# The first expert's list taken from its counts again, and two digits of the second search ahead of the expert matmuls

## The chip, the cores and the metric

The kernel runs on one core of a Trainium2 chip. The metric is the device time of one execution in microseconds (us): the median of three runs. The engines are TensorE (PE in the profile, PEld for its weight loads), VectorE (DVE), ScalarE (ACT), GpSimd (POOL), and SyncE (SP), which issues DMAs here.

## The reference, cut to what matters

Two blocks, one behind the other. The first is a linear recurrence over 768 steps for 4 batches and 8 heads of 48 elements. Its output, 3072 tokens of 384 elements, goes to a layer of eight experts, in which every expert takes exactly 384 tokens. The tokens are given out greedily: all 3072 x 8 scores are sorted, and each token goes to its best expert that still has a place.

```python
def _moe_ref(x, w_gate, w1, w2):
    N, D = x.shape                      # 3072, 384
    E = w_gate.shape[1]                 # 8
    cap = N // E                        # 384
    logits = x @ w_gate
    order = np.argsort(-logits.flatten())
    assigned = -np.ones(N, dtype=np.int64)
    counts = np.zeros(E, dtype=np.int64)
    for idx in order:
        tok, e = (int(idx) // E, int(idx) % E)
        if assigned[tok] >= 0 or counts[e] >= cap:
            continue
        assigned[tok] = e
        counts[e] += 1
        ...
    for e in range(E):
        mask = assigned == e
        h = np.maximum(x[mask] @ w1[e], 0.0)
        out[mask] = h @ w2[e]
```

## The kernel before: the parts concerned

The attention block runs in steps, with the routing's constants made beside it in small pieces. Then the kernel fills one expert in each round. A round searches for the level of the score at which the first expert is full, in five digits of four bits, from the highest to the lowest; gives that expert its tokens; makes a list of them; gathers their rows; and queues that expert's matmuls. The expert matmuls of the list before are taken from the queue `pe_work` in small portions, between the search's own small matmuls, so that TensorE isn't idle while VectorE works. In the first round there is nothing queued, and idle matmuls (`idle_turns`) stand in the gaps.

A digit is counted in one of two ways. `digit_alone` needs 24 small matmuls (4 in the first round's first digit) and few operations of VectorE. `digit_beside` needs 3 matmuls and one more, and more operations of VectorE, and takes expert matmuls from the queue in two portions, `slots`.

```python
def digit_alone(above, parts, choice, unit, counted=None, turns=(0, 0), scored=None):
    some(pe_work, turns[0])
    r = bank("cnt", "r")
    ...                                            # the counts: 24 matmuls
    fills = rt([E], "fills", BF16)
    tt(fills[0:NTH, :], r[0:NTH, 0:E], ..., ALU.is_ge)
    filled = rt([1], "filled", BF16)
    reduce(filled[0:NTH, :], fills[0:NTH, :], ALU.max)
    if turns[1]:
        some(pe_work, turns[1])
        idle_turns(2, bank("nothing", "O"))
    digit = r[:, 128:129]
    nc.tensor.matmul(out=digit, lhsT=unit[0:NTH, :], rhs=filled[0:NTH, :], start=True, stop=True)
    if scored:
        scores, n = scored
        nc.tensor.matmul(out=scores[:, 0:E], lhsT=weights[n][:], rhs=fills[0:NTH, :],
                         start=(n == 0), stop=(n == len(weights) - 1), skip_group_check=True)
    return digit, ALU.add

def digit_beside(above, choice, size, slots):
    some(pe_work, slots[0])
    ...                                            # cnt: 3 matmuls
    some(dve_work, 1)
    ...                                            # own, part, parts
    some(pe_work, slots[1])
    ...                                            # cnt: 1 matmul; fillsb, filledb, sized and digit
```

After the search the expert's tokens are marked. The first round does it in its own way, the others with `assign`:

```python
def assign(choice, over, pick, slots):
    over, level = over
    stt(sure[:], col(over[:], E), level, choice[:], ALU.is_ge, ALU.mult)
    reduce(count[:], by_e(sure), ALU.add)
    some(pe_work, slots[0])
    r = bank("sums", "r")
    nc.tensor.matmul(out=r[:, 0:E], lhsT=ones[:], rhs=count[:], start=True, stop=True)
    some(pe_work, slots[1])
    take(over[:], pick, level)                     # new, taken
    tt(places[:], places[:], r[:, 0:E], ALU.subtract)

def assign_first(choice, over, pick, scores):
    over, level = over
    reduce(top[:], scores[:, 0:E], ALU.max)
    stt(named[:], scores[:, 0:E], top[:], first[:], ALU.is_equal, ALU.mult)
    reduce(m[:], named[:], ALU.max)
    stt(taken[:], over[:], level, pick[:], ALU.is_ge, ALU.mult)
    def marked():
        stt(sure[:], col(over[:], E), level, choice[:], ALU.is_ge, ALU.mult)
    def counted():
        ...                                        # count, its matmul (sums), places
    return m, marked, counted
```

The list: `members` names the expert that is full (m) and its tokens, `place` numbers them, `index` computes the number e, on which the load of the weights depends, `lines` and `in_line` sort the tokens into lines, and `tokens` ends in three gathers by GpSimd. The first list's rows (xe) are transposed by TensorE into xeT; those of the later lists by DMA, between copies of GpSimd.

```python
def members():
    ...
    named = m
    if named is None:
        stt(score[:], places[:], 0.5, left[:], ALU.is_lt, ALU.mult)
        reduce(named[:], score[:], ALU.max)
    ts(member[:], taken[:], named[:], ALU.is_equal)

for rnd in range(E - 1):
    slots, more = pace.get(rnd, (4, 2)), 3 if rnd > 1 else -2 if rnd and not exact else 0   # pace: rounds 1, 2: (3, 2)
    ...
    scores = bank("scores", "H") if rnd == 0 else None
    over = search(choice, over, digits, slots, more, counted, ((1, 1),) if rnd == 1 else (), scores)
    if rnd or exact:
        (assign_exact if exact else assign)(choice, over, pick, (3, 3))
        *pieces, used = expert_list(rnd == 0)
    else:
        m, marked, after = assign_first(choice, over, pick, scores)
        *pieces, tokens, used = expert_list(True, m=m)
        pieces += [marked, tokens, after]
    dve_work.extend(pieces)
    while dve_work:
        some(dve_work, 1)
        if rnd: some(pe_work, 1)
        elif dve_work: idle_turns(1, bank("nothing", "O"))
    close()                                        # full, penalty
    if rnd == 0:
        idle_turns(13, bank("nothing", "O"))
        dve_work.append(lambda: also(bank("hits", "r")))   # the range check, taken up in the next search
```

Of the kernel before, what the change touches and what calls it, by code (L numbers as in the profile page):

```python
# [11 lines left out]
FP32 = mybir.dt.float32  # L12
FP32R = mybir.dt.float32r
BF16 = mybir.dt.bfloat16
# [13 lines left out]
def kernel(  # L28
# [32 lines left out]
    nc = tc.nc  # L61
# [520 lines left out]
    taken = rt([NT], "taken", FP32, 1)  # L582

    lowest = rt([E], "lowest", FP32, 1)
    lowlogit, digits, weights = const([128, 1], FP32, "lowlogit"), [], []

    def bounds(c1):

# [36 lines left out]
        def table(shift):  # L625
            steps = const([128, NTH], FP32, f"steps_{shift}")
            ts(steps[:], count[:, 0:NTH], step[:], ALU.mult, float(1 << shift), ALU.mult)
            unit = const([128, 128], BF16, f"unit_{shift}")

            ts(unit[:], ones[:], step[:], ALU.mult, float(1 << shift) * (-1 if shift else 1),  # L630
               ALU.mult)
            digits.append((steps, unit, steps[:, 0:1]))
            weight = const([NTH, 128], BF16, f"weight_{shift}")
            nc.vector.memset(weight[:], float(1 << shift))
            weights.append(weight)

        def negated():
            ts(pair[:, 1:2], pair[:, 1:2], -1.0, ALU.mult)
# [81 lines left out]
    def assign_and_run(begun=None, also=None, again=None, exact=None):  # L720
# [57 lines left out]
            else:  # L778
                stt(above[:, c0:c1], over, digit, steps, op, ALU.is_ge)

        def digit_alone(above, parts, choice, unit, counted=None, turns=(0, 0), scored=None):

            some(pe_work, turns[0])
            r = bank("cnt", "r")
            cols = [c for c in range(NT) if not counted or c % NCH == NCH - 1]
            for c in cols:
                if c % 8 == 0 and not counted:
                    parts(c, c + 8)
                nc.tensor.matmul(out=r[0:NTH, 0:E], lhsT=above[:, c, :], rhs=choice[:, c, :],
                                 start=(c == cols[0]), stop=(c == cols[-1]))  # L790
# [52 lines left out]
        def search(choice, over, digits, slots, first=0, counted=None, alone=(), scores=None):  # L843


            def less(over, digit, op):
# [7 lines left out]
            for n, (steps, unit, size) in enumerate(digits):  # L854
                above = counted[0] if counted else rt([NT, NTH], "above", BF16)
                parts = partial(reached, above, over, digit, op, steps)
                if slots and n >= len(alone):
                    parts(0, NT)
                    new = less(over, digit, op)
                    digit, op = digit_beside(above, choice, size, (slots[0] + first, slots[1]))  # L860
                    over = new
                else:
                    new, op_new = digit_alone(above, parts, choice, unit, counted,
                                              *(alone[n:n + 1] or ((0, 0),)),
                                              scored=(scores, n) if scores is not None else None)
                    over = less(over, digit, op)
                    digit, op = new, op_new
                if n >= len(alone):
                    first = 0
                counted = None  # L870
            return less(over, digit, op) if exact else (over, digit)

        def assign(choice, over, pick, slots):
# [10 lines left out]
            some(pe_work, slots[1])  # L884
            take(over[:], pick, level)
            tt(places[:], places[:], r[:, 0:E], ALU.subtract)

        def assign_first(choice, over, pick, scores):

            over, level = over  # L890
            top, named, m = rt([1], "top_"), rt([E], "named"), rt([1], "m")
            reduce(top[:], scores[:, 0:E], ALU.max)
            stt(named[:], scores[:, 0:E], top[:], first[:], ALU.is_equal, ALU.mult)
            reduce(m[:], named[:], ALU.max)
            stt(taken[:], over[:], level, pick[:], ALU.is_ge, ALU.mult)
            sure = rt([NT, E], "sure", BF16)

            def marked():
                stt(sure[:], col(over[:], E), level, choice[:], ALU.is_ge, ALU.mult)

            def counted():
                count = rt([E], "count", BF16)
                with nc.allow_low_precision("counts of at most 24"):
                    reduce(count[:], by_e(sure), ALU.add)
                r = bank("sums", "r")
                nc.tensor.matmul(out=r[:, 0:E], lhsT=ones[:], rhs=count[:], start=True, stop=True)
                tt(places[:], places[:], r[:, 0:E], ALU.subtract)

            return m, marked, counted

        def assign_exact(choice, over, pick, slots):
            def take_all(mask):
# [39 lines left out]

            stt(wanted[:], full[:], 2.0 * N, places[:], ALU.mult, ALU.add)

        def expert_list(alone=False, last=False, m=None):

            L = {"place": next(turns), "last": last}

# [6 lines left out]
            def members():  # L965
                if alone:

                    L["xe"] = [rows() for _ in range(TE)]
                    for xe in L["xe"]:
                        nc.gpsimd.memset(xe[0:1, 0:1], 0.0)  # L970
                named = m
                if named is None:
                    score, named = rt([E], "score"), rt([1], "m")
                    stt(score[:], places[:], 0.5, left[:], ALU.is_lt, ALU.mult)
                    reduce(named[:], score[:], ALU.max)
                member = rt([NT], "member")
                ts(member[:], taken[:], named[:], ALU.is_equal)
                L.update(member=member, m=named)

            def place():  # L980
                incl = rt([NT], "mincl", BF16)
# [189 lines left out]
        with tc.manual_schedule(engines=engines):  # L1171
# [3 lines left out]

            pace, settle = {0: None, 1: (3, 2), 2: (3, 2)}, []
            for rnd in range(E - 1):
                slots, more = pace.get(rnd, (4, 2)), 3 if rnd > 1 else -2 if rnd and not exact else 0
                if exact:
                    best, pick, masked = picks()  # L1180
                    choice = choices_exact(pick, masked)
# [11 lines left out]
                else:  # L1193
# [234 lines left out]
```

## Time and profile before

| what | value |
|---|---|
| median of 3 runs | 449.82 us (449.33 to 450.61) |
| span in the profile | 448.2 us |
| mean granted TensorE clock | 0.979 |
| TensorE busy | 426.6 us, 95% |
| VectorE busy | 274.0 us, 61% |
| DMA | 63.25 MB, mean 141 GB/s |

The page divides the span into 40 slices of 11.2 us. A digit is the busy share of a slice in tenths; PEclk is the granted TensorE clock in the same way.

```profile
PE   8999999999999678998999999999999999999994
DVE  6789977778987677766666567567567562000000
PEclk9999999999999859999999999999999999999999
```

Thirteen slices are the attention. In the next two or three, where the first list is searched and made, TensorE has little to do and its clock falls; the rest is the experts' matmuls with the later searches among them. The largest groups of instructions are the two kinds of expert matmuls (L1141 and L1153), 264 us together.

### The profile page before, as it was taken

The numbers are of one execution on the slowest core, as the hardware profiler recorded it, in microseconds if no ns is written. First come the engines' busy times: TensorE is split into PE (matmuls) and PEld (weight loads), VectorE is DVE, ScalarE is ACT, GpSimd is POOL, SyncE is SP. The second block draws the span as 40 slices with busy tenths as digits, with TensorE's granted clock in tenths as the row PEclk, the third lists the DMA queues.
The fourth block names the chain that finished last, engine by engine and source line by source line (L and its number), as shares of the span: only waits on it lengthen the run. The fifth ranks groups of instructions, "written<-read, shape, count | busy, mean of one in ns | idle before, by whom it ended". The sixth has DMA issues, their size and how long they took to land. (4 is left out here: it accounts for less than half of the span.)

```text
span 448.2 us, 11779 instructions
## 1 busy us (share of the span) xinstructions
PE 426.6 (95%) x4806; PEld 287.2 (64%) x4806; DVE 274.0 (61%) x887; ACT 129.3 (29%) x302; POOL 174.9 (39%) x231
## 2 busy tenths in 40 slices
PE   8999999999999678998999999999999999999994
PEld 5788988898888535554565565565565565555552
DVE  6789977778987677766666567567567562000000
ACT  4666665666552101200210210210210211211210
POOL 2566555565551021036146037037037037531001
PEclk9999999999999859999999999999999999999999
DMA  9999998999811136084194093093093096820001
GB/s 158 180 165 191 195 189 181 207 196 199 182 38 39 37 114 221 1 303 99 38 333 72 35 335 86 20 332 78 31 333 88 19 332 169 293 56 35 0 20 39
DMA packets 135200, 63.25 MB, mean 141 GB/s; under 512 B 118464, under 2 KB 129760, under 8 KB 135136
## 3 DMA queue, kind: packets, MB, share of 16 engines
q1 hardware_dynamic: 132016, 52.91, 47.6%
q0 software_dynamic: 3072, 9.44, 5.8%
q8 instruction: 40, 0.66, 0.6%
q14 instruction: 24, 0.20, 0.1%
q10 hardware_dynamic: 48, 0.05, 0.1%
HBM read 48.77 MB, written 9.49 MB: 130 GB/s over the span
## 5 line engine op out<-in xcount | busy, mean ns | idle before, releaser
L1141 PE MATMUL H<-xeT,w 128*128 128x384 f32 x384 | 131.9, 495 | 1.6 <-POOL xeT L1110 1.5
L1141 PEld LDWEIGHTS H<-xeT,w 128*128 128x128 f32 x384 | 69.3, 190 | 45.9 <-issue 5.4
L1153 PE MATMUL O<-w,hT 128*128 128x384 f32 x192 | 66.5, 492 | 0.0
L1153 PE MATMUL last_O<-w,hT 128*128 128x384 f32 x192 | 66.1, 491 | 0.0
L1145 ACT ACTIVATE hT<-H 128x384 f32<-128x384 f32 x64 | 31.4, 491 | 104.2 <-PE H L1141 102.8
L1153 PEld LDWEIGHTS last_O<-w,hT 128*128 128x128 f32 x192 | 35.4, 190 | 22.6 <-issue 0.9
L1153 PEld LDWEIGHTS O<-w,hT 128*128 128x128 f32 x192 | 35.1, 190 | 22.9 <-issue 2.0
L327 DVE COPY_PREDICATED am<-mask,A 128x512 f32<-128x512 int32 x48 | 32.2, 724 | 17.5 <-PE A L322 17.5
L193 POOL TENSOR_TENSOR low<-g,upper 128x384 fp32r<-128x384 f32 x22 | 22.3, 1013 | 43.4 <-DVE upper L191 40.2
L1030 POOL TENSOR_TENSOR block<-past 128x72 f32<-128x72 f32 x8 | 2.5, 306 | 88.3 <-DVE at L570 77.5
L1072 POOL DMA_INDIRECT xe<-xd,token x21 | 21.4, 1020 | 26.1 <-DVE full L567 15.8
L337 PE MATMUL Y<-v,am 128*64 128x48 f32 x768 | 27.8, 223 | 1.2 <-DVE am L327 1.1
L1158 POOL DMA_INDIRECT out_dram<-o,token x21 | 21.8, 1037 | 16.9 <-ACT o L1157 12.8
L1110 POOL COPY xeT<-cols 128x768 uint16<-128x768 uint16 x21 | 22.2, 1066 | 14.0 <-DMA cols<-parts 13.9
L337 PEld LDWEIGHTS Y<-v,am 128*64 128x64 f32 x768 | 24.8, 138 | 2.3 <-DVE am L327 1.9
L246 POOL TENSOR_TENSOR kg<-k,ek 128x384 f32<-128x384 f32 x23 | 23.1, 1004 | 7.2 <-ACT ek L224 5.4
L322 PE MATMUL A<-qT,kT 48*64 48x128 f32 x768 | 25.7, 272 | 0.0
L1100 POOL COPY parts<-xe 128x768 uint16<-128x768 uint16 x21 | 17.4, 855 | 17.0 <-DMA xe<-xd,token 14.4
L1157 ACT COPY o<-O 128x384 f32<-128x384 f32 x12 | 5.7, 479 | 61.1 <-PE O L1153 45.5
L223 ACT ACTIVATE eq<-dl 128x384 f32<-128x384 f32 x24 | 12.5, 523 | 31.7 <-DVE dl L221 31.7
L1157 ACT COPY o<-last_O 128x384 f32<-128x384 f32 x11 | 5.3, 479 | 55.3 <-PE last_O L1153 35.5
L322 PEld LDWEIGHTS A<-qT,kT 48*64 48x64 f32 x768 | 20.9, 133 | 0.4 <-issue 0.3
(238 smaller groups left out, 683.3 us busy)
## 6 DMA issues: line engine op xcount, KB each, us to landing
w<-in_moe_w_dram SPq DMA_DIRECT2D x16, 1536.0 KB, 7.0
f<-in_f_logit_dram SPq DMA_DIRECT2D x24, 192.0 KB, 4.0
q<-in_q_dram SPq DMA_DIRECT2D x24, 192.0 KB, 4.6
k<-in_k_dram SPq DMA_DIRECT2D x24, 192.0 KB, 4.7
v<-in_v_dram SPq DMA_DIRECT2D x24, 192.0 KB, 4.7
xd<-x SPq DMA_DIRECT2D x24, 192.0 KB, 3.8
xe<-xd,token POOLq DMA_INDIRECT x21, 4.9
cols<-parts SPq DMA_TRANSPOSE x21, 2.8
```

What stands on the lines that cost most here:

```text
L193: nc.gpsimd.tensor_tensor(out=low[:], in0=g[:, :, 0:DH], in1=upper[:].bitcast(FP32), op=ALU.subtract)
L246: engine.tensor_tensor(out=G["kg"][:, :, 0:DH], in0=G["k"][:], in1=G["ek"][:], op=ALU.mult)
L322: nc.tensor.matmul(out=A[par][HC * j:HC * j + HC, 128 * hp:128 * hp + 128], lhsT=G["kT"][rows, hp, HC * j:HC * j + HC], rhs=G["qT"][rows, ...
L327: nc.vector.copy_predicated(am[:, par], mask[:].unsqueeze(1).to_broadcast((128, HP, 128)), A[par][:].rearrange("s (a t) -> s a t", t=128))
L337: nc.tensor.matmul(out=Y[par][HC * j:HC * j + HC, DH * hp:DH * hp + DH], lhsT=G["am"][:, par, hp, HC * j:HC * j + HC], rhs=G["v"][:, 2 * h ...
L1072: nc.gpsimd.indirect_dma_start(out=xe[:], out_offset=None, in_=xd[:, :], in_offset=bass.IndirectOffsetOnAxis(ap=token[:, i:i + 1], axis=0))
L1100: nc.gpsimd.tensor_copy(out=rows[-1][:], in_=xe[:].bitcast(U16).rearrange("t (d h) -> t h d", h=2))
L1110: nc.gpsimd.tensor_copy(out=halves[:, :, :, 128 * i:128 * i + 128], in_=t[:].rearrange("p (h c) t -> p h c t", h=2))
L1141: nc.tensor.matmul(out=L["H"][:, 0:CAP], lhsT=L["w1"][:, d, 128 * ft:128 * ft + 128], rhs=xT[:, d, :], start=(d == 0), stop=(d == DC - 1))
L1145: nc.scalar.activation(out=hT[:, ft, :], in_=L["H"][:, 0:CAP], func=AF.Relu)
L1153: nc.tensor.matmul(out=L["O"][:, 0:D], lhsT=hT[:, ft, 128 * i:128 * i + 128], rhs=L["w2"][:, ft, :], start=(ft == 0), stop=(ft == FC - 1))
L1158: nc.gpsimd.indirect_dma_start(out=outs[next(tiles)][:, :], out_offset=bass.IndirectOffsetOnAxis(ap=L["token"][:, i:i + 1], axis=0), in_=o ...
```

## The change

The change takes the first list's special way out. The first round's expert is no longer named from sums of the digits' comparisons (`scores`, with the five constants `weight`), but as in the later rounds from the places that are left, which `assign` counts ahead of the list; so the counting stands ahead of the list again and not behind it. In the second round two digits of the search are counted with `digit_alone`, with the portions (0, 1) and (1, 1) of the queue, where before it was one with (1, 1); and the third digit takes 3 + 2 from the queue, where before the second took 3 - 2 = 1 and then 2. What it is for: fewer parts and one way for all rounds, and one digit less among the expert matmuls.

```diff
-    lowlogit, digits, weights = const([128, 1], FP32, "lowlogit"), [], []
+    lowlogit, digits = const([128, 1], FP32, "lowlogit"), []
...
-            weight = const([NTH, 128], BF16, f"weight_{shift}")
-            nc.vector.memset(weight[:], float(1 << shift))
-            weights.append(weight)
...
-        def digit_alone(above, parts, choice, unit, counted=None, turns=(0, 0), scored=None):
+        def digit_alone(above, parts, choice, unit, counted=None, turns=(0, 0)):
...
-            fills = rt([E], "fills", BF16)
+            fills = rt([E], "fills")
...
-            if scored:
-
-                scores, n = scored
-                nc.tensor.matmul(out=scores[:, 0:E], lhsT=weights[n][:], rhs=fills[0:NTH, :],
-                                 start=(n == 0), stop=(n == len(weights) - 1),
-                                 skip_group_check=True)
...
                     new, op_new = digit_alone(above, parts, choice, unit, counted,
-                                              *(alone[n:n + 1] or ((0, 0),)),
-                                              scored=(scores, n) if scores is not None else None)
+                                              *alone[n:n + 1])
...
-                if n >= len(alone):
-                    first = 0
-                counted = None
+                first, counted = 0, None
...
-        def assign_first(choice, over, pick, scores):
-            ...                                                   (the whole function)
...
-                named = m
-                if named is None:
-                    score, named = rt([E], "score"), rt([1], "m")
-                    stt(score[:], places[:], 0.5, left[:], ALU.is_lt, ALU.mult)
-                    reduce(named[:], score[:], ALU.max)
+                score, m = rt([E], "score"), rt([1], "m")
+                stt(score[:], places[:], 0.5, left[:], ALU.is_lt, ALU.mult)
+                reduce(m[:], score[:], ALU.max)
...
-                slots, more = pace.get(rnd, (4, 2)), 3 if rnd > 1 else -2 if rnd and not exact else 0
+                slots, more = pace.get(rnd, (4, 2)), 3 if rnd > 1 else 0
...
-                    scores = bank("scores", "H") if rnd == 0 else None
                     over = search(choice, over, digits, slots, more, counted,
-                                  ((1, 1),) if rnd == 1 else (), scores)
-                if rnd or exact:
-                    (assign_exact if exact else assign)(choice, over, pick, (3, 3))
-                    *pieces, used = expert_list(rnd == 0)
-                else:
-                    m, marked, after = assign_first(choice, over, pick, scores)
-                    *pieces, tokens, used = expert_list(True, m=m)
-                    pieces += [marked, tokens, after]
+                                  ((0, 1), (1, 1)) if rnd == 1 else ())
+                (assign_exact if exact else assign)(choice, over, pick, (3, 3))
+                *pieces, used = expert_list(rnd == 0)
```

In the order of TensorE's instructions the change moves these: the five matmuls for `scores` go; the matmul for `sums` moves from behind the tokens to ahead of the list; 24 small count matmuls, two idle matmuls and one digit's matmul come in among the three transposes of the first list's rows; and the range check's matmul (`hits`) stands behind three expert matmuls instead of ahead of all.

More of the change, by code (lines that the diff above doesn't have):

```diff
@@ L841, in digit_beside, with search @@
             return digit[:], ALU.subtract
-        def search(choice, over, digits, slots, first=0, counted=None, alone=(), scores=None):
+        def search(choice, over, digits, slots, first=0, counted=None, alone=()):
             def less(over, digit, op):
@@ L886, in assign @@
             tt(places[:], places[:], r[:, 0:E], ALU.subtract)
-        def assign_first(choice, over, pick, scores):
[L890 to L909, printed above, removed]
         def assign_exact(choice, over, pick, slots):
@@ L953, in closed, with expert_list @@
             stt(wanted[:], full[:], 2.0 * N, places[:], ALU.mult, ALU.add)
-        def expert_list(alone=False, last=False, m=None):
+        def expert_list(alone=False, last=False):
             L = {"place": next(turns), "last": last}
@@ L970, in members @@
                         nc.gpsimd.memset(xe[0:1, 0:1], 0.0)
-                named = m
-                if named is None:
-                    score, named = rt([E], "score"), rt([1], "m")
-                    stt(score[:], places[:], 0.5, left[:], ALU.is_lt, ALU.mult)
-                    reduce(named[:], score[:], ALU.max)
+                score, m = rt([E], "score"), rt([1], "m")
+                stt(score[:], places[:], 0.5, left[:], ALU.is_lt, ALU.mult)
+                reduce(m[:], score[:], ALU.max)
                 member = rt([NT], "member")
-                ts(member[:], taken[:], named[:], ALU.is_equal)
-                L.update(member=member, m=named)
+                ts(member[:], taken[:], m[:], ALU.is_equal)
+                L.update(member=member, m=m)
             def place():
```

## The prediction

> **What bounds the kernel now.** The page's busy table comes first: TensorE is busy for 95% of the span, VectorE for 61%. The chain that ended last says nothing here (it covers only the last queue's closing steps), so the stages have to be cut by hand from the slices and then measured with the table of windows. Its columns are span, busy time and count of PE, PEld, DVE, ACT and POOL, then granted clock, DMA share and GB/s.
>
> ```profile
> PE 426.6 (95%) x4806; PEld 287.2 (64%) x4806; DVE 274.0 (61%) x887; ACT 129.3 (29%) x302; POOL 174.9 (39%) x231
> ...
> 160.40:166.20 5.80, 4.04 (x33) 1.45 (x34) 5.32 (x20) 0.00 (x0) 1.29 (x2) 0.50 0.30 82
> 166.20:175.00 8.80, 7.13 (x58) 3.95 (x56) 6.41 (x29) 1.44 (x3) 3.32 (x4) 0.81 0.91 321
> 175.00:209.30 34.30, 34.02 (x147) 19.31 (x146) 23.87 (x90) 4.96 (x11) 8.42 (x10) 1.00 0.45 140
> 209.30:210.90 1.60, 0.08 (x1) 0.08 (x1) 1.49 (x3) 0.40 (x1) 1.47 (x2) 1.00 0.05 10
> 210.90:440.00 229.10, 228.28 (x912) 132.51 (x913) 108.48 (x400) 37.09 (x76) 83.01 (x89) 1.00 0.42 134
> ```
>
> From 210.9 us on TensorE has no hole to speak of: the end follows the start of the second expert's first matmul one for one. Three things set that start: the end of the attention (about 150 us), the first list's way to its first expert matmul (150 to 175 us), and the hole at 209.3 us. The timeline shows the last two; columns are start, duration, engine, line and operation, and what ended the idle time ahead.
>
> ```profile
> 160.44 0.17 DVE L573 TENSOR_REDUCE top__3687<-scores 128x1 f32<-128x8 f32 x1
> 161.25 0.24 DVE L567 TENSOR_SCALAR member<-taken,m 128x24 f32<-128x24 f32 x1
> 165.77 0.16 DVE L570 SCALAR_TENSOR_TENSOR token<-pair 128x3 int32<-128x3 f32 x1
> 167.21 0.18 DVE L567 TENSOR_SCALAR full<-places 128x8 f32<-128x8 f32 x1
> 173.37 0.48 ACT L1133 COPY xeT<-Xe 128x384 f32<-128x384 f32 x1 [0.43 <-PE Xe L1130]
> 174.84 0.19 PE L1291 MATMUL hits<-onesf,span 128*1 128x1 f32 x2 [1.00 <-DVE span L570]
> 174.96 0.59 PE L1141 MATMUL H<-xeT,w 128*128 128x384 f32 x1
> 195.73 0.75 PE L1057 MATMUL tokens<-number,in_line 128*128 128x6 bf16 x24
> 210.82 1.56 PE L1141 MATMUL H<-xeT,w 128*128 128x384 f32 x4 [1.55 <-POOL xeT L1110]
> ```
>
> Two losses are to be seen. The first expert's inputs were ready at 173.37 + 0.48 = 173.85 us, yet its first matmul began at 174.96, because the range check's matmul (hits) stands ahead of it in program order and waits for VectorE. And the second expert waits 1.55 us for its rows (xeT), whose list was made too late.
>
> [...] hits held H back for 1.1 us. [...] clock 0.50 in 160.4 to 166.2 us, and the weight loads of the idle matmuls are 0.32 us apart until 169.51, 0.16 after it. [...] The three gathers hold GpSimd for 1.19, 1.09 and 0.95 us, one behind another.
>
> **The change part by part.**
>
> (a) Five memsets (weight) leave the attention stage. They start 0.10 us ahead of their successors (114.26 to 114.36), and VectorE has no idle time from 108.7 to 132 us, where the tables are made. The copies of xT, one in each attention step, are 5.5 to 6.0 us apart before, then 6.24 and 6.22 in the two steps with two tables and 5.63 in the one with one table, and TensorE waits 0.20 + 0.28 us for am in the second. VectorE sets the pace there. 5 x 0.10 = 0.5 us less, of which TensorE gets perhaps 0.4, as VectorE then idles again for A. Worth -0.4 us, all of which moves what follows.
>
> (b) Five matmuls (scores) leave the first search. Each lies behind the digit matmul, in time in which TensorE waits for VectorE (0.42 us each time). Worth nothing.
>
> (c) The way from the last digit to member. Before: top at 160.44 to member at 161.25. After, it is the way of the second round, which the trace has: sure at 188.05, member at 189.87, so 1.82 us. The last digit's matmul starts at 160.21 and its reader 0.20 later (as at 154.44 and 154.64), at 160.41; member then starts at 162.23, 0.98 later than before. All of place, index, lines, the tokens and the first gather shift by +0.98.
>
> (d) What stood behind the tokens goes: before, token at 165.77 to full at 167.21 is 1.44 us (count, its matmul, places). In the second round that step is 0.08 (196.72 to 196.80). So the second search starts 0.98 - 1.36 = -0.38 us, that is earlier, its first comparison at 170.48 instead of 170.86.
>
> (e) The second search's second digit is counted in 24 small matmuls ahead of the first expert's matmuls, instead of beside them. In (c) to (e) times are without the -0.4 of (a). The first count starts at 170.48 + 0.34 = 170.82, if the 14 idle matmuls ahead are done. From count to digit 1.49 us as before (171.20 to 172.69): 172.34. The next count 0.61 later (152.51 to 153.12): 172.95. Third gather landed: before at 169.12 + 3.1 = 172.2, now 173.2. The third transpose stands behind the second count, 172.95 + 0.7 = 173.65; its copy by ScalarE is done 1.06 later (172.79 to 173.85), at 174.7; the second digit at 172.95 + 1.49 = 174.45. So the first expert matmul could start at 174.8; with a clock that rises late I allow 175.2, and take 175.0. The hits matmul now stands behind three expert matmuls (1.9 us), by when span is done. So the whole +0.98 is swallowed: 175.0 against 174.96.
>
> (f) The second list. One digit less is searched between the expert matmuls: before 2 and three times 3 + 2, so 17 expert matmuls to the end of the search, after three times 5, so 15. Behind it all is the same. One expert matmul (two rows of the trace) takes 0.645 us (5.16 for 8). So its tokens come 2 x 0.645 = 1.29 us earlier seen from the first expert matmul: 20.77 - 1.29 = 19.5 behind it. From tokens to the second expert's first matmul it took 210.82 - 195.73 = 15.1 us, so its rows are ready 34.6 us behind the first expert matmul. TensorE itself needs 209.27 - 174.96 = 34.3 us for the first expert with what is between; that count of small matmuls stays six pairs, plus hits, so 34.4. The hole of 1.55 shrinks to 0.2 and the second expert starts at 175.0 + 34.6 = 209.6 instead of 210.82: -1.2 us.
>
> Sum: -0.4 - 1.2 = -1.6 us. The later lists had slack before and gain two expert matmuls more, so nothing is given back there.
>
> **The rivals.**
>
> The first: the +0.98 us isn't swallowed. Then the first expert matmul starts at about 175.9 and everything behind it too, the hole stays at 0.2, and the routing gains 0.3 us only: with (a) 449.1. For it: the third gather and the third transpose are both near the path. Against: 1.1 us of wait behind hits is there to be used.
>
> The second: the clock. [...] An expert matmul at half rate costs 0.645 us more, [...] and the time goes to about 451. For it: more small matmuls with waits between them now lie ahead of the first expert matmul. Against: the 14 idle matmuls are still in one run, as the 13 before, at about the same time.
>
> The third: VectorE's slow operations beside GpSimd's copies. One comparison took 1.22 instead of 0.62 us at 204.22, one product 0.99 instead of 0.29 at 209.87. The product's matmul now stands directly ahead of the second expert's first matmul, so such a delay could add up to 0.7 us. But GpSimd's last copy of xeT ends the same stretch, so most of it hides in the hole that is left: with all of it 448.9.
>
> The fourth: (a) yields nothing, because the last attention steps are paced by TensorE: 448.6.
>
> **Range and chances.** 449.82 - 1.6 = 448.2. Three of the four rivals end above that and none below, so I move the point up by 0.3: 448.5 us. The low end takes a first expert matmul at 174.5 and all of (a), 447.3; the high end 450.3 holds the first rival and a half of the second, and the spread of the runs before (449.33 to 450.61). 2% is 9 us; nothing here has that size: faster 0.01, same 0.98, slower 0.01.
>
> **What will show it.** (a) VectorE's step over two tables 6.0 instead of 6.2 us, the attention's end 0.4 earlier. (c) sure to member 1.82 us. (e) hits without the wait of 1.00, first expert matmul within 0.4 us of 175.0 less the shift of (a). (f) tokens of the second list 19.5 us behind it and the wait for xeT at 0.2 to 0.5 us. I am wrong if the wait for xeT is still over 1 us, if the first expert matmul comes a microsecond later, or if the granted clock behind it is under 1.

## The result and the profile after

The changed kernel takes 447.83 us (447.78 to 448.15, 4 runs), the kernel before, measured with it, 449.97 us. The ratio is 0.9954, 95% interval 0.9937 to 0.9971. A second comparison with more runs (a2_again below) gives 0.9971 (0.9958 to 0.9984). So the change is worth 1.3 to 2.1 us, 0.3 to 0.5%; 448.5 us had been predicted.

The table of windows of the changed kernel, cut at the same events as before (columns: span, then busy time and count of PE, PEld, DVE, ACT and POOL, then clock, DMA share, GB/s):

```profile
159.90:166.70 6.80, 4.79 (x37) 1.86 (x37) 5.89 (x24) 0.00 (x0) 1.94 (x3) 0.50 0.32 114
166.70:174.50 7.80, 7.66 (x76) 4.50 (x75) 5.37 (x25) 1.43 (x3) 2.52 (x4) 0.80 0.92 310
174.50:208.50 34.00, 33.64 (x147) 19.14 (x146) 24.30 (x91) 4.88 (x10) 9.41 (x11) 1.00 0.49 145
208.50:440.00 231.50, 229.99 (x917) 133.17 (x915) 109.80 (x401) 37.97 (x78) 83.33 (x91) 1.00 0.41 133
```

The hole of 1.6 us has no window of its own any more. In 166.7 to 174.5 us TensorE is busy for 7.66 of 7.80 us; before it was 7.13 of 8.80. The timeline of the changed kernel (start, duration, engine, line and operation, what ended the idle time ahead):

```profile
159.24 0.42 DVE L570 SCALAR_TENSOR_TENSOR sure<-over,cnt,choice 128x192 bf16<-128x192 f32 x1
161.07 0.24 DVE L567 TENSOR_SCALAR member<-taken,m 128x24 f32<-128x24 f32 x1
165.59 0.16 DVE L570 SCALAR_TENSOR_TENSOR token<-pair 128x3 int32<-128x3 f32 x1
165.67 0.16 DVE L567 TENSOR_SCALAR full<-places 128x8 f32<-128x8 f32 x1
...
169.95 0.75 PE L786 MATMUL cnt<-choice,above 128*16 128x8 bf16 x24
173.98 2.20 PE L1104 MATMUL H<-xeT,w 128*128 128x384 f32 x6
176.20 0.19 PE L1248 MATMUL hits<-onesf,span 128*1 128x1 f32 x2
...
193.60 0.75 PE L1020 MATMUL tokens<-number,in_line 128*128 128x6 bf16 x24
...
209.07 0.22 PE L822 MATMUL cnt<-parts,ones 128*128 128x128 bf16 x1 [0.30 <-DVE parts L563]
209.17 1.21 PE L1104 MATMUL H<-xeT,w 128*128 128x384 f32 x3
```

Most of the signs that the prediction named can be looked up here: sure to member 161.07 - 159.24 = 1.83 us; token to full 0.08; hits now behind six rows of H and without a wait; tokens 193.60 - 173.98 = 19.62 behind the first expert matmul; and the second expert's first matmul without a wait for xeT. It now has the matmul of the sums (L822) ahead of it, which waits 0.30 for VectorE.

Where the profile's 2.5 us lie (us, each interval from the two traces; the first row starts at the attention's first transposes, 8.74 and 8.75 us; "attention's end" is VectorE's first need, where the routing begins, 151.58 and 150.43 us):

| from, to | before | after | difference |
|---|---|---|---|
| first transposes to the table step (111 us) | 102.96 | 102.07 | -0.89 |
| table step to attention's end | 39.88 | 39.61 | -0.27 |
| attention's end to first expert matmul | 23.38 | 23.55 | +0.17 |
| first to second expert | 35.86 | 35.19 | -0.67 |
| second to seventh expert | 167.09 | 166.74 | -0.35 |
| seventh to eighth expert | 32.50 | 31.96 | -0.54 |
| eighth expert | 31.12 | 31.12 | 0.00 |

The first row isn't the change's. In the profiled execution of the kernel before, one attention step (65.0 to 71.6 us), whose instructions both kernels have alike, took 0.88 us longer. The timeline shows 0.35 of it as a wait of TensorE, and puts it down to nothing but issue:

```profile
70.57 0.36 PE L391 MATMUL X<-wg,xT 128*64 128x8 f32 x7
71.28 0.34 PE L391 MATMUL X<-wg,xT 128*64 128x8 f32 x5 [0.35 <-issue]
```

The same interval took 102.03 to 103.21 in the kernels below, without order; it is a chance of the one profiled execution. What is left, 1.66 us, is of the size that the medians show, 1.3 to 2.1.

### The profile page after: what moved, and what is told of

It reads as the page before. It is cut to its first block, busy times and chain, and to the rows that moved or that the text cites. A ratio compares the mean times of both kernels' runs of the same rounds, so it can differ in the third digit from the quotient of the medians.

```text
span 445.7 us, 11801 instructions
## 1 busy us (share of the span) xinstructions
PE 426.9 (96%) x4822; PEld 287.5 (65%) x4822; DVE 273.9 (61%) x879; ACT 129.2 (29%) x302; POOL 174.5 (39%) x231
```

## The experiments

The theory at the start: the gain comes from the second list (the digit searched ahead of the first expert), with a little from the memsets; the first list's new way is worth nothing. The rivals: the gain is in the first list's way, or in hits alone, or in the memsets alone. Four kernels, each with one part. On their chip the kernel before took 449.74 us.

**e1_search: the changed second search alone, put into the kernel before.**

```diff
-  slots, more = pace.get(rnd, (4, 2)), 3 if rnd > 1 else -2 if rnd and not exact else 0
+  slots, more = pace.get(rnd, (4, 2)), 3 if rnd > 1 else 0
...
-      ((1, 1),) if rnd == 1 else (), scores)
+      ((0, 1), (1, 1)) if rnd == 1 else (), scores)
```

> The kernel before, with the changed second search alone (two digits counted ahead of the expert matmuls); the first list is still named from the sums, the five memsets stay. Theory (the gain lies in the second search, the way of the first list costs nothing because its microsecond is hidden): first expert matmul at about 175.1 us by the clock of the profile before (174.96 there), wait for xeT 0 to 0.4 us, time 448.5 us, 1.4 under the kernel before and 0.3 over the changed kernel. Rival (the gain comes from taking the first list's special way out): time within 0.3 us of the kernel before, 449.9.

Measured: 449.2 us, ratio 0.9991 (0.9979 to 1.0002). The second list comes as predicted: tokens 19.61 us behind the first expert matmul, first to second expert 34.75 us, which is 1.11 less than before (predicted: 1.2), no wait for xeT. How much of the 1.11 is the search's own, e3_memsets tells. Ahead of it the first expert matmul came 0.42 later (23.80 us behind the attention's end), and later lists gave another 0.3 back. Net 0.4 us by the trace.

**e2_list: the changed kernel with the old second search**, that is the first list's way and the memsets without the rest.

```diff
-                first, counted = 0, None
+                if n >= len(alone):
+                    first = 0
+                counted = None
...
-  slots, more = pace.get(rnd, (4, 2)), 3 if rnd > 1 else 0
+  slots, more = pace.get(rnd, (4, 2)), 3 if rnd > 1 else -2 if rnd and not exact else 0
...
-      ((0, 1), (1, 1)) if rnd == 1 else ())
+      ((1, 1),) if rnd == 1 else ())
```

> The changed kernel, with the second search as before (one digit ahead, 1 + 2 from the queue). Theory: the list's 0.98 us now shows in part, first expert matmul about 0.5 us later than before, hits again waits for VectorE ahead of it, the wait for xeT is back at about 1.5 us; less the memsets the time is 450.2, at most 0.4 us from the kernel before. Rival (the gain comes from taking the special way out): 448.0.

Measured: 449.78 us, ratio 1.0005 (0.9987 to 1.0022). Nothing, against the rival's 448.0. In its trace the first expert matmul is 0.52 us later and hits waits 1.0 us again, as expected, but the wait for xeT is 0.45 us and not 1.5.

**e3_memsets: the kernel before, with the five constants filled by GpSimd in an early attention step.**

```diff
+    weights = []
+    for shift in SHIFTS:
+        weight = const([16, 128], BF16, f"weight_{shift}")
+        nc.gpsimd.memset(weight[:], float(1 << shift))
+        weights.append(weight)
...
-            nc.vector.memset(weight[:], float(1 << shift))
```

> The kernel before, with the five memsets of weight given to GpSimd in the third attention step, so that VectorE is rid of them in the stretch of 110 to 128 us. Theory: the attention ends 0.3 us earlier (what the two profiles show between 109.9 and 150 us) and the time falls by 0.3 to 449.7. First rival: TensorE sets the pace, no difference. Second rival: the 0.88 us by which the changed kernel is ahead at 104 us comes from the memsets too, time 448.8.

Measured: 449.28 us, ratio 0.9988 (0.9976 to 1.0001). The trace settles the size in the attention: table step to attention's end takes 39.63 us, 0.25 less. All the kernels here that have the memsets on VectorE show 39.85 to 39.88, all without 39.60 to 39.63. VectorE's copies of xT show the pace, first before, then changed:

```profile
116.16 0.53 DVE L383 COPY xT<-X 128x384 f32<-128x384 f32 x1
122.38 0.53 DVE L383 COPY xT<-X 128x384 f32<-128x384 f32 x1
128.01 0.52 DVE L383 COPY xT<-X 128x384 f32<-128x384 f32 x1
```

```profile
115.18 0.55 DVE L383 COPY xT<-X 128x384 f32<-128x384 f32 x1
121.32 0.53 DVE L383 COPY xT<-X 128x384 f32<-128x384 f32 x1
126.86 0.53 DVE L383 COPY xT<-X 128x384 f32<-128x384 f32 x1
```

6.22 became 6.14 with two memsets gone, 5.63 became 5.54 with one: 0.04 to 0.09 us for a memset, not 0.10.

But the memsets did more than that. With the search unchanged, first to second expert takes 35.14 us in e3_memsets instead of 35.86, and the wait for xeT is 0.68 us instead of 1.55. TensorE's waits, 166 to 213 us:

```profile
PE H L1143 <- POOL xeT L1112: 0.7, 1, 0.7
```

So 0.72 of the 1.11 us that e1_search gained there also come with the old search; how that comes about is taken up below. The first expert matmul, too, is 0.49 later than in the kernel before (23.87 us behind the attention's end), though nothing near it was changed: the kernel before's 23.38 was an early one.

**e4_hits: the kernel before, with the range check's matmul behind the first two expert matmuls.** VectorE's part stays where it was.

```diff
                     if also:
+                        dve_work.append(also)
                         dve_work.append(lambda: also(bank("hits", "r")))
...
+        if r is not None:
+            ...                                    # the matmul and the copy, as below
+            return
...
-        nc.tensor.matmul(out=r[0:1, 0:1], lhsT=span[:], rhs=onesf[:], start=True, stop=True)
-        nc.vector.tensor_copy(out=beyond[:], in_=r[0:1, 0:1])
```

> The kernel before, with the range check's matmul (hits) behind the first two expert matmuls and their sums; VectorE's part of the check stays where it was. Theory: the first expert matmul starts 1.0 us earlier, at 173.9, but VectorE's check delays the next digit, so that the second list gains 0.7 and the wait for xeT stays at 1.4; time 449.3, 0.7 less. Rival (the wait behind hits is the whole loss): 448.9. Other rival (the second list alone decides and doesn't move): no difference.

Measured: 449.9 us, ratio 1.0000 (0.9986 to 1.0014). The first expert matmul does come 1.0 us earlier (22.39 behind the attention's end), but less than half of that reaches the second list: its tokens come 0.43 us earlier. TensorE's waits in the stretch from 166 to 212 us, e4_hits:

```profile
PE H L1141 <- POOL xeT L1110: 1.5, 1, 1.5
PE cnt L816 <- DVE above L570: 0.4, 2, 0.2
```

The wait of 1.0 for span is gone, the wait for xeT is as long as before, and first to second expert takes 36.28 us instead of 35.86. The list sets the start of the second expert here, not TensorE's work. That start is still 0.58 us earlier, and this is lost further on: the second expert to TensorE's last matmul takes 231.72 us instead of 230.71.

No part alone gave what the whole gives. So the changed kernel was measured again, with three variants of the stretch around the first list. On that chip the kernel before took 449.5 us.

**a2_again: the changed kernel once more.**

> The changed kernel itself, once more, timed beside the four kernels of the first set's kind: do its 2.1 us hold over more runs? The stages of the profiles so far give: memsets 0.26, first expert matmul 0.17 later seen from the attention's end, from there to the second expert 35.1 to 34.8 us where the DMA's transposes land in their usual 2.8 us; together 0.5 us, more only where a transpose lands late in the kernel before. First theory (the stages are all there is): 0.5 to 1.0 us under the kernel before. Second theory (the first comparison holds): 1.5 to 2.5 us under it.

Measured: 448.43 us (22 runs), ratio 0.9971. The profile has a surprise: this execution does wait 1.1 us for xeT, and tokens to second expert takes 16.00 us, where the kernel before took 15.09. A wait for xeT of over 1 us was one of the prediction's signs of being wrong.

**t1_turns: the queue's portions in another turn**, (0, 2), (1, 0) for (0, 1), (1, 1).

> The changed kernel, with the second search's portions (0, 2) and (1, 0): the third transpose stands ahead of the second count and the second pair of idle matmuls is gone. Theory (the second search's two counts set the first expert matmul, the gathers have slack): first expert matmul 0.25 us earlier seen from the attention's end (23.3 instead of 23.55 us), time 0.25 less than the changed kernel. Rival (the gathers set it): the transposes wait for their rows, the count behind them too, 0.3 us later.

Measured: 448.51 us, ratio 0.9978 (0.9965 to 0.9991): the changed kernel's time. The first expert matmul came 23.44 us behind the attention's end, not 23.3.

**t2_idle: 11 idle matmuls instead of 13 behind the first list's tokens.**

> The changed kernel with 11 idle matmuls in place of 13 ahead of the second search. In its profile the first count waited about 0.35 us behind idle matmuls that ran at half rate. Theory: first expert matmul 0.35 us earlier, 23.2 us behind the attention's end, the clock rises at the same time; time 0.35 less than the changed kernel. Rival (the clock): [...] the counts or the first expert matmuls run at half rate, the time rises by 0.5 to 3 us.

Measured: 448.77 us, ratio 0.9982 (0.9965 to 0.9999). The second search's first count came 0.29 us earlier behind token (4.07 for 4.36), and from there to the first expert matmul it took 0.15 longer: in this execution the clock rose 0.55 us into the count, in the changed kernel's 0.11 ahead of it. By the medians nothing comes of it.

**t3_both: t1_turns and t2_idle.**

> The two before together. Theory: the two gains add up to 0.6 us, first expert matmul 22.95 us behind the attention's end, and all behind it moves with it. Rival (the second list is then late again): the first expert matmul gains 0.6 us, but the wait for xeT grows by as much and the time stays.

Measured: 449.0 us, ratio 0.9991 (0.9968 to 1.0015). First count to first expert matmul took 5.17 us instead of 4.03, because the clock rose only 0.9 us ahead of the first expert matmul (at 174.55 us), in the changed kernel 4.1 us ahead.

What these runs showed, and nobody had expected, is the landing of the second list's three DMA transposes. These four profiles, and the first one of the changed kernel, have it. The view of the tile cols in the second list, first e3_memsets, then the changed kernel (issue durations in ns, starts in us, then issue to landing):

```profile
L1108 SPq DMA_TRANSPOSE cols<-parts x3: 1265/1287/1332, 203.5 to 206.2; - x3
...
DMA to landing us min/median/max: 2.8/2.8/2.8
```

```profile
L1069 SPq DMA_TRANSPOSE cols<-parts x3: 1264/1287/1332, 201.0 to 203.7; - x3
...
DMA to landing us min/median/max: 2.8/3.8/4.5
```

The same instruction on the same tiles lands up to 1.7 us later. The DMA view of the changed kernel, 203 to 206 us (queue, packets, MB, share of 16 engines), names a second customer:

```profile
q1 hardware_dynamic: 1440, 0.35, 99.5%
q8 instruction: 1, 0.02, 2.2%
```

One packet of 16 KB in a queue that the view names instruction, right among the transposes. All 40 packets of this queue have that size in the kernel before and in the changed one. It is taken here for TensorE's program being fetched, because five matmuls more in that program moved it by 2.95 us in each of two runs below (p1_pad, p3_pad_before). So a second theory: the place of this fetch decides when the second list lands. In the changed kernel it comes 11.05 us behind the list's tokens, the transposes are issued from 7.4 to 10.1 us behind them and land by 13.9. In e1_search, whose TensorE program is five matmuls and five weight loads longer ahead of that point (scores), it comes at 6.98, ahead of all. (Of e1_search's three landings the trace has only the second, 2.8 us; GpSimd took up the third tile 3.3 us behind its issue.) The rival: the transposes are late because the list comes earlier, beside other transfers. Two kernels to move the fetch out of the way, one to move it in, and one for the part still missing; the kernel before took 449.84 us on their chip.

**p1_pad: the changed kernel with five small matmuls in the first search**, in time in which TensorE waits.

```diff
                                               *alone[n:n + 1])
+                    if slots is None and not exact:
+                        for _ in range([1, 1, 1, 1, 1][n]):
+                            nc.tensor.matmul(out=bank("nothing", "O")[:, 0:8], lhsT=ones[:],
+                                             rhs=idle[:, 0:8], start=True, stop=True)
                     over = less(over, digit, op)
```

> The changed kernel with five small matmuls (128x8, result unread) in the first search, one behind each digit while TensorE waits for VectorE: TensorE's program is ten instructions longer ahead of the second list, nothing else differs. Theory (the place of TensorE's 16 KB instruction fetch decides when the second list's transposes land): the fetch moves from 11.1 us behind the second list's tokens to about 7, the three transposes land in 2.8 us each in place of 2.8/3.8/4.5, tokens to second expert matmul takes 15.15 us or less in place of 15.6 to 16.1, and the time is 0.4 to 0.9 us under the changed kernel's, a ratio near 0.996. Rival (the transposes are late because the list comes earlier, beside other transfers): fetch or no fetch, they land in 3.8 to 4.5 us and the time is the changed kernel's.

Measured: the fetch moved to 8.10 us behind the tokens. The view of cols in p1_pad's second list:

```profile
L1073 SPq DMA_TRANSPOSE cols<-parts x3: 1266/1287/2007, 201.2 to 204.5; - x3
...
DMA to landing us min/median/max: 2.8/2.8/3.2
```

Tokens to second expert took 15.22 us, 0.35 to 0.78 less than in the two profiles of the changed kernel. So far the theory. But the time is 449.1 us, ratio 0.9979 (0.9961 to 0.9996), not 0.996: what is won there isn't in the end. The trace shows where most of it went: the fourth expert to the fifth takes 34.00 us instead of 33.44, the fifth to the sixth 33.81 instead of 33.44. The timeline of p1_pad, TensorE, VectorE, GpSimd:

```profile
304.08 0.22 PE L822 MATMUL cnt<-parts,ones 128*128 128x128 bf16 x1 [0.40 <-DVE parts L563]
302.90 1.12 DVE L563 TENSOR_TENSOR parts<-part,pick_th 128x128 bf16<-128x128 bf16 x1
302.90 1.04 POOL L1077 COPY xeT<-cols 128x768 uint16<-128x768 uint16 x1 [1.03 <-DMA cols<-parts]
```

The same product in the changed kernel:

```profile
303.61 0.29 DVE L563 TENSOR_TENSOR parts<-part,pick_th 128x128 bf16<-128x128 bf16 x1
303.66 2.31 POOL L1073 COPY xeT<-cols 128x768 uint16<-128x768 uint16 x2 [1.06 <-DMA cols<-parts]
```

GpSimd's copy and VectorE's product begin in the same 10 ns, and the product takes 1.12 us for 0.29; TensorE waits. In the changed kernel the product began 0.05 us ahead of the copy and wasn't slowed. That the shift of the second list brought this meeting about is likely but not shown.

**p2_pad_turns: t1_turns with seven such matmuls.**

> The portions taken in the turn of t1_turns, with seven small matmuls in the first search (two, two, one, one, one behind the digits). Fetch theory: the fetch moves to about 7 us behind the second list's tokens or ahead, tokens to second expert matmul 15.15 us or less, and the time 0.25 us under p1_pad, the least of all: about 0.995 of the kernel before. Rival: the transposes stay at 3.8 to 4.5 us and the time is that of t1_turns, 0.998.

Measured: 449.09 us, ratio 0.9976 (0.9958 to 0.9994), the changed kernel's time. The profiled execution has the fetch at 8.67, among the transposes and not ahead of them. The issue of the second one took 2.30 us instead of about 1.3, so that the third was issued at 11.1 us behind the tokens, and they landed in 3.8 to 4.3:

```profile
L1073 SPq DMA_TRANSPOSE cols<-parts x3: 1287/1332/2296, 203.5 to 207.3; - x3
```

It lost another 1.7 us at the start of the first expert. Its windows there:

```profile
174.84:180.00 5.16, 5.16 (x16) 2.77 (x16) 2.62 (x11) 0.49 (x1) 0.00 (x0) 0.67 0.36 132
180.00:185.00 5.00, 5.00 (x21) 2.87 (x20) 3.24 (x14) 0.98 (x2) 0.00 (x0) 1.00 0.00 0
```

The granted clock was 0.67 over the first 5 us of the expert: it had risen at 168.34 us, and from 175.17 to 178.58 it was at half once more. The expert's first six rows took 3.88 us, six rows from 180.31 us on 2.15. That is akin to the prediction's second rival; in the changed kernel's own profile it is 1.00 there.

**p3_pad_before: the kernel before with five such matmuls**, the reverse test.

> The kernel before with five small matmuls in the first search, one behind each digit: the reverse test. Fetch theory: the fetch moves from 14.1 us behind the second list's tokens to 10.5 or 11, into the transposes, which land in 3.8 to 4.5 us in place of 2.9 to 3.8; the second expert matmul's wait for xeT grows from 1.55 to 1.6 to 2.2 us or more, and the time from the kernel before's by 0.3 to 0.8 us. Rival: padding TensorE's program moves nothing, ratio 1.000 within 0.001.

Measured: 451.18 us, ratio 1.0026 (1.0006 to 1.0046): slower, by five matmuls that stand in idle time. The fetch moved from 14.10 to 11.15 us behind the tokens. The cols of the second list, first the kernel before, then p3_pad_before:

```profile
L1106 SPq DMA_TRANSPOSE cols<-parts x3: 1267/1292/1332, 203.5 to 206.2; - x3
...
DMA to landing us min/median/max: 2.9/3.1/3.8
```

```profile
L1110 SPq DMA_TRANSPOSE cols<-parts x3: 1264/1332/2219, 203.4 to 206.1; - x3
...
DMA to landing us min/median/max: 2.8/4.5/5.2
```

TensorE's waits from 166 to 213 us in p3_pad_before, and the windows behind them:

```profile
PE H L1145 <- POOL xeT L1114: 2.9, 1, 2.9
```

```profile
212.12:217.00 4.88, 4.88 (x11) 2.63 (x12) 1.58 (x6) 0.49 (x1) 2.99 (x3) 0.69 0.33 121
217.00:222.00 5.00, 5.00 (x22) 2.83 (x21) 3.15 (x12) 0.98 (x2) 0.00 (x0) 1.00 0.00 0
```

The wait for xeT went from 1.55 to 2.93 us, where 1.6 to 2.2 or more was expected, and behind it the mean clock was 0.69 for 4.9 us: the second expert took 35.18 us for 33.59. That is 1.4 + 1.6 us in the profiled execution; the medians show 1.3, where 0.3 to 0.8 was expected. The 16 KB fetch was not alone there: a fetch of 8 KB (queue q14) came at 11.48 us. The kernel before has that one too, at 11.61 us, which is where its own 3.8 us come from.

The packets in the trace show how a fetch delays a transpose. Each transpose ends with 32 packets of 4 bytes. In the changed kernel 30 of the second transpose's had come by 11.14 us behind the tokens, the other two at 12.34, right behind the fetch's own packet, which took from 11.05 to 12.10. In p4_rest all 32 came between 10.99 and 11.20. Two of 32 is what would wait if the packets were spread evenly over the 16 DMA engines of the profile and the fetch kept one of them busy; that is an estimate from these counts, and which engine it was, the trace doesn't say. The kernel before has the same with its 8 KB fetch, which took from 11.61 to 11.92: 30 of the second transpose's last packets had come by 11.53, the other two came at 11.92.

The 8 KB fetch explains what e3_memsets gained at the second list. In the four profiled kernels that have the memsets on VectorE it comes 11.47 to 11.74 us behind the tokens, in the ten others 13.13 to 13.79, at the end of the transposes or behind them. So the change moved two fetches: this one out of the way, with the memsets (from 11.61 to 13.52 us behind the tokens), and the one of 16 KB into it (from 14.10 to 11.05).

**p4_rest: the changed kernel except for the first list's way**, that is e1_search with the memsets of e3_memsets.

> The changed kernel except for the first list's way: the kernel before with the changed second search and with the memsets on GpSimd. It tells the first list's way (the removal of the sums over slots and the wait of 1.00 ahead of hits, paid with 0.98 ahead of the first list) from the rest. Theory (the first list's way is worth nothing by itself): time 0.26 us under e1_search, about 0.9985 of the kernel before, the changed kernel's within 0.6 us. Rival (the way to the first list carries the gain): it stays 1 us or more above the changed kernel, at 1.000 of the kernel before.

Measured: 449.15 us, ratio 0.9988 (0.9975 to 1.0000). That is the theory's number (0.9985), though not a clear verdict: it is 0.13 us under e1_search in these terms, not 0.26, and by the medians 0.8 us above a2_again, with intervals that overlap. In the trace its fetch (7.10) is out of the way, its transposes land in 2.8, and the first to the second expert takes 34.74 us. By the end it stands 0.97 us better than the kernel before from the attention's end on, the two profiles of the changed kernel 1.39 and 1.19, and e3_memsets, with nothing but the memsets moved, 0.83.

## Why the prediction was right, and where not

The time and the range held. The working held up to the second list's tokens; behind them two steps failed, in opposite directions, and that they nearly cancel was luck.

(a), memsets, -0.4: right in kind, too large. It is about 0.26 us in every kernel without them, as the operation behind a memset then takes longer itself (steps 0.40 us before, 0.54 after). That the memsets also moved a fetch, worth 0.7 us at the second list in e3_memsets, is in no part of the prediction.

(b), "worth nothing": right in its own stretch: attention's end to the last digit is 8.6 us with and without. But p1_pad and p3_pad_before show that five matmuls in idle time aren't neutral later: they shifted TensorE's fetch by 2.95 us in each, and with it the transposes' landings.

(c) and (d): right. sure to member is 1.83 us (1.82), member comes 0.99 later behind the last digit (0.98), token to full is 0.08.

(e), the first expert matmul: predicted 0.04 later than before, measured 0.17 later. "If the 14 idle matmuls ahead are done" was the weak place: the count begins at 169.95, when the run of idle matmuls ends, and VectorE's fills waits 0.73 us for it. Against the other kernels with the old first list and an unmoved hits (e1_search, e3_memsets, p3_pad_before and p4_rest: 23.69 to 23.87 us behind the attention's end) the changed kernel's 23.55 is early. The small sums of (e) hold a slip: 170.82 + 1.49 is 172.31, not 172.34. The rest of (e) holds: hits doesn't wait, the granted clock behind is 1.00.

(f), the second list: tokens 19.62 us behind (19.5): right. The first step that failed is "from tokens to the second expert's first matmul it took 15.1 us, so its rows are ready 34.6 us behind". In the two profiles of the changed kernel it took 15.57 and 16.00 us. In the second, the transposes landed in 4.2 to 4.5 us and the second expert waited 1.12 us for xeT. In the first, GpSimd's last copy of xeT ended 15.3 us behind the tokens, and the matmul of the sums held the second expert for the rest: VectorE's product for it took 1.02 us beside GpSimd's copies. Counted from the attention's end, the second expert starts 0.50 and 0.10 us earlier than before, not 1.2.

The prediction took the transposes' landing as fixed, from a profile in which a fetch had already made it late. Where they land in 2.8 to 2.9 us, first to second expert takes 35.14 and 35.05 us with the old search (e3_memsets, e2_list) and 34.74 with the new one (p4_rest), so that the search itself is worth 0.3 to 0.4 us. That TensorE's fetch decides the landing is shown by p3_pad_before and p1_pad, in which only the padding moved it and the landings went with it both ways (2.8 to 4.5 us became 2.8 to 3.2 in p1_pad, 2.9 to 3.8 became 2.8 to 5.2 in p3_pad_before).

The second step that failed is "the end follows the start of the second expert's first matmul one for one", with "nothing is given back there". From the second expert's start to TensorE's last matmul it took 230.71 us before and 229.83 and 229.62 in the changed kernel, and between 229.60 and 231.72 in all profiles. So the later lists gained 0.9 to 1.1 us, about as much as the second list fell short. One place where they did is the last list. Its tokens wait for GpSimd's number, which stands behind three scatters of the output. First before, then changed:

```profile
382.63 0.75 PE L1057 MATMUL tokens<-number,in_line 128*128 128x6 bf16 x24 [0.58 <-POOL number L1032]
```

```profile
378.81 0.74 PE L1020 MATMUL tokens<-number,in_line 128*128 128x6 bf16 x24 [0.15 <-POOL number L995]
```

Seventh to eighth expert took 31.96 or 31.97 us in all seven profiled kernels with the whole change, and 32.2 to 32.8 in six of those with a part of it or none. p3_pad_before, without the change, has 31.94, so it may be how the scatters fall and not the change's order of work; that was seen, not tested.

The rivals. The first (0.98 not swallowed) fell: attention's end to the first expert is +0.17. The second (clock), whose 451 was an estimate, didn't happen in the changed kernel's profile and did, in one form or the other, in t3_both and p2_pad_turns. The third happened in part: in its profile two matmuls of the sums, the second of them just ahead of the second expert, waited 0.24 and 0.30 us for VectorE's parts. The fourth fell by e3_memsets' trace. By the prediction's own figures (449.1, 451, 448.9, 448.6) all four end above 448.2, not three of them.

On the parts: search alone 0.9991, list alone with memsets 1.0005, all but the list 0.9988, all 0.9954 and 0.9971. By the medians the search with the old memsets, the memsets alone (0.9988) and both together can't be told apart, and none of them from no gain with certainty. What is shown is that the whole change gains, that the second list's tokens come 1.16 us earlier behind the first expert matmul, and that the landing of its rows, which fetches move, decides how much of that is left. Which part carries the rest, and whether the list's way adds the last 0.2 to 0.8 us, stays open.

## What to carry to other kernels

A wait taken away just ahead of the work only helps as far as what follows moves with it: e4_hits moved the first expert 1.0 us, the second 0.6 and the end not at all. When a list's transfers are near the path, look in the DMA view for the packets of the instruction queues: here five matmuls more in the first search moved one by 2.95 us, out of the transfers in p1_pad and into them in p3_pad_before, where the wait behind them grew by 1.4 us. A 1 us effect in one profile may be that and not the change. And before crediting a change with a difference, cut both traces at common events: here a third of it lay in code that both kernels share. A part's gain, too, needs a second base to be read against: of e1_search's 1.11 us, 0.72 came also without its search.

## What the hardware showed beyond that

- DMA transposes of one shape land in 2.8 us with no instruction fetch among them (e3_memsets, p4_rest), in up to 3.8 us with one of 8 KB (the kernel before), up to 4.5 with one of 16 KB (the changed kernel), and up to 5.2 with both (p3_pad_before). Part of the hole that the change removes was made by that: with the memsets alone moved, the wait for xeT was 0.68 us instead of 1.55.
- A pause of TensorE of 2.93 us cost another 1.6 us by the clock (0.69 over the next 4.9 us), one of 1.55 us nothing (1.00 over the next 4.9 us in the kernel before). In the longer one the clock fell at 211.73 us, 2.54 us into it, and rose 3.41 us later. In p2_pad_turns it fell at 175.17 us, for 3.41 us too, although the profile has TensorE busy for 2.74 of the 3.41 us ahead and its longest wait there was 0.43 us; what set the fall off was not shown.
- Five matmuls of 128x8 in idle time made a kernel 0.26% slower (p3_pad_before).
